# First pair's q and k in 1536-byte rows, turned by products with the identity, its clusters in two halves

## Chip, cores and metric

The kernel runs on one core of a Trainium2 chip. The metric is the device time of one execution in microseconds (us), the median of several runs; "profiled execution" means one further run that the hardware profiler recorded. The engines are TensorE (PE; its weight loads are listed apart as PEld), VectorE (DVE), ScalarE (ACT), GpSimd (POOL) and SyncE (SP), which issues most DMAs.

## What is computed

Attention in which a query sees only the keys of its own cluster, followed by a mixture of experts in which each token goes to one expert. Shapes: 4 batches, 8 heads, 768 tokens, head width 64, 16 centroids per head; the attention's output, as 3072 rows of 512, goes to 8 experts (512 to 1024 to 512).

```python
q_assign = argmax(einsum('bhsd,hcd->bhsc', q_n, c_n)); k_assign likewise   # unit vectors
mask   = q_assign[:, :, :, None] == k_assign[:, :, None, :]
scores = where(mask, q @ k.T / sqrt(64), -1e9)
attn   = softmax(scores) @ v                       # reshaped to x: (3072, 512)
logits = x @ w_gate; e = argmax(logits); gate = softmax(logits)[e]
out    = gate * (relu(x @ w1[e]) @ w2[e])
```

## The kernel before

**Attention.** The 32 (batch, head) pairs are done two heads at a time: 16 "pairs", numbered n. Each has 768 tokens, worked on as two halves of 384 query columns (h = 0, 1) and six blocks of 128 keys (j = 0 to 5). For a pair:

- `load(n)` fetches q and k, `load_v(n)` fetches v. For n > 0 the rows come as quarters of 32 that `turn` (L277, DVE, 32 x 32 block transposes) turns into qT and kT, head width along the partitions, tokens along the columns. For n = 0 the tokens come in another layout, with DMAs on SP and ACT (L183), and PE turns them by 12 transposes (L267); `first_turn` copies the result out of PSUM (L282), half by DVE and half by ACT.
- `similar` (L312, PE): products with the normalised centroids cT (made at L248 to L257 from `cin`, turned by PE at L270, copied at L291).
- `assign0` to `assign2` (L325 to L348, DVE, seven instructions): the largest similarity of each token, ties to the first, as a one-hot row `ohT`.
- `place(n, 1)` (L361, DVE, four instructions) writes the keys' one-hot rows, scaled by a huge number and shifted, into `mk`; `place(n, 0)` (L359, ACT, for n = 0 also POOL) copies the queries' into `mq`. A product of mk and mq adds 0 where the clusters agree and a huge negative number elsewhere.
- `score(n, h, j)`: `score_half` twice on PE (L379), first kT with qT in fp32, then mk with mq in bf16 into the same PSUM tile `sps` (three such tiles); then ACT's exp into A (L392). Before the first score of all, three fp32 halves are issued ahead.
- `add_up` (L398, DVE) sums A over j, `attend` (L404, PE) multiplies by v, `sum_up` (L427, PE) makes the row sums and the gate's logits from `wgt`, `rows` and `store` write x out.

**Order.** Within the attention part each engine runs its instructions in the order in which the program writes them. The main loop, for each n, issues the loads of n + 2, then the twelve scores; after score u (u = h * 6 + j) it calls what a table, filled by `at_pair(n, u, ...)`, holds for that place: the preparation of pair n + 1 in five steps (1 similar, 2 assign0 and assign1, 3 assign2, 4 place keys, 5 place queries), and the work left from pair n - 1. Then come the products with v, in whose middle DVE turns q and k of pair n + 2. Pair 0's five steps run ahead of the loop, one after the other. `routing_constants` (POOL memsets, and SP's DMAs that fill `tokens_of` from `none`, L141) comes after them.

**SP's queue before**: q, k of pair 0 (half of each; ACT issues the other halves, and `cin` and `wgt`); the store of the centroids `c_normed` (waits for cT); v of pair 0; q, k, v of pair 1; eight `tokens_of`; loads of pair 2.

**Experts.** The second part gathers rows by expert and multiplies them in fp32 (L916, L1017, L1036). The change doesn't touch it.

Of the kernel before, what the change touches and what calls it, by code (L numbers as in the profile page):

```python
# [8 lines left out]
F32 = mybir.dt.float32  # L9
BF16 = mybir.dt.bfloat16  # L10
# [3 lines left out]
ALU = mybir.AluOpType  # L14
# [19 lines left out]
def kernel(  # L34
# [45 lines left out]
    cn_d = nc.dram_tensor("c_normed", (H, D, C), F32, kind="Internal").ap()  # L80
# [82 lines left out]
    with tc.manual_schedule(), ExitStack() as actx:  # L163
# [96 lines left out]
        first = []  # L260
        cps = ps_m.tile([P, 512], F32, name="mps")
        for d in (QIN, KIN):
            ps = ps_s.tile([P, 2, 512], F32, name="sps")
            t = d.pop(0)
            for j in range(NQ):
                c0 = P * (j % 3)
                nc.tensor.transpose(ps[:, j // 3, c0 : c0 + P], t[:, j].rearrange("p a d -> p (a d)"), ident)  # L267
            first.append(ps)
            if d is QIN:
                nc.tensor.transpose(cps[:, 0:P], cn.rearrange("p a d -> p (a d)"), ident)  # L270

        QT, KT, SIM, OH = {}, {}, {}, {}

# [2 lines left out]
            dst[n] = qkt.tile([P, S], F32, name=name)  # L276
            nc.vector.transpose(dst[n], src.pop(n).rearrange("p i d -> p (i d)"))  # L277

        def first_turn(w):
            t = (QT, KT)[w][0] = qkt.tile([P, S], F32, name=("qT", "kT")[w])  # L280
            for ins in (
                nc.vector.tensor_copy(t[:, 0:HS], first[w][:, 0, 0:HS]), nc.scalar.copy(t[:, HS:S], first[w][:, 1, 0:HS])  # L282
            ):
                ins = getattr(ins, "ins", ins)
                tc.declare_no_dep(ins, group=f"first_turn{w}", reason="disjoint columns")
                tc.add_to_no_dep_group(f"first_turn{w}", ins)

        first_turn(0)
        cv = cps[:, 0:P].rearrange("p (h a c) -> p h a c", a=2, c=C)
        for a in range(2):  # L290
            nc.vector.tensor_copy(cT[D * a : D * (a + 1), :, a, :], cv[D * a : D * (a + 1), :, a, :])  # L291
        for a in range(2):
            nc.sync.dma_start(
                out=cn_d.rearrange("(h a) d c -> a d h c", a=2)[a], in_=cT[D * a : D * (a + 1), :, a, :]
            )

        load_v(0)
        load(1)
        first_turn(1)
        first_cb = consts.tile([P, C], BF16)  # L300
        nc.gpsimd.tensor_copy(first_cb, first_c)
        ksc2 = consts.tile([P, 2], F32)
# [14 lines left out]
                )  # L317
            SIM[n] = ps

        G = 2 * HI  # L320

        def assign0(n):

            sim = asg.tile([P, HI, 2 * C], F32, name="sim")
            nc.vector.transpose(sim.rearrange("p i c -> p (i c)"), SIM.pop(n)[:, 0:HS])  # L325
            SIM[n] = sim.rearrange("p i (a c) -> p (i a) c", c=C)

        def assign1(n):
            sim = SIM[n]
            mx = asg.tile([P, G], F32, name="mx")  # L330
            nc.vector.tensor_reduce(mx, sim, axis=AX, op=ALU.max)
            ge = asg.tile([P, G, C], BF16, name="ge")
# [3 lines left out]
        def assign2(n):  # L336
            ge = SIM.pop(n)
            rank = asg.tile([P, G, C], BF16, name="rank")
            nc.vector.tensor_tensor(rank, ge, first_cb[:, None, :].to_broadcast([P, G, C]), op=ALU.mult)
            top = asg.tile([P, G], BF16, name="top")  # L340
            nc.vector.tensor_reduce(top, rank, axis=AX, op=ALU.max)
            oh = asg.tile([P, HI, 2 * C], BF16, name="oh")
# [4 lines left out]
            OH[n] = asg.tile([P, HS], BF16, name="ohT")  # L347
            nc.vector.transpose(OH[n], oh.rearrange("p i c -> p (i c)"))  # L348

        def place(n, w):  # L350
            t, m = OH[n], (MQ, MK)[w][n % 2]
            for h in range(2):
                for a in range(2):
                    g = 2 * w + h
                    dst = m[D * a : D * a + Q4, HS * h : HS * (h + 1)]
                    src = t[Q4 * g : Q4 * (g + 1), :]
                    if w == 0:

                        (nc.gpsimd.tensor_copy if n == 0 and h else nc.scalar.copy)(dst, src)  # L359
                    else:  # L360
                        nc.vector.tensor_scalar(  # L361
                            dst, src, scalar1=ksc2[Q4 * g : Q4 * (g + 1), a : a + 1],
                            scalar2=kscn2[Q4 * g : Q4 * (g + 1), a : a + 1], op0=ALU.mult, op1=ALU.add,
                        )
            if w == 0:
                OH.pop(n)


        A, ACC, O, OT, SL = {}, {}, {}, {}, {}
# [3 lines left out]
        def score_half(n, h, j, first):  # L373
            if first:
                SP[n, h, j] = ps_s.tile([P, 2, 512], F32, name="sps")
            kt, qt = (KT[n], QT[n]) if first else (MK[n % 2], MQ[n % 2])
            for a in range(2):
                rows = slice(D * a, D * (a + 1))
                nc.tensor.matmul(  # L379
                    SP[n, h, j][:, a, 0:HS], lhsT=kt[rows, j * P : (j + 1) * P], rhs=qt[rows, h * HS : (h + 1) * HS],  # L380
                    start=first, stop=not first,
                )

        def score(n, h, j):

            ahead = range(3) if n + h + j == 0 else (j,) if n + h or j > 2 else ()
            for i in ahead:
                score_half(n, h, i, True)
# [3 lines left out]
            nc.scalar.activation(A[n, h, j], ps[:, :, 0:HS], AF.Exp, scale=D**-0.5)  # L392
# [1067 lines left out]
```

## Time and profile before

| what | us |
|---|---|
| three timed runs | 671.42, 668.75, 671.11 (median 671.11) |
| the profiled execution's own time | 672.25 |
| its span, from first to last instruction | 670.7 |
| PE busy / DVE busy / ACT busy / POOL busy | 649.9 / 512.3 / 300.0 / 127.3 |
| mean granted TensorE clock | 0.992 |
| one pair in the steady state (first product with v to the next pair's) | 19.74 |

The profile's page gives each engine's busy time, the chain of work that ended last, and the costliest groups of instructions. Lines of the order of time read: start, length, engine, source line, operation, tile written <- tiles read, shape, count, and in brackets the idle time of the engine before it and what ended it. Matmuls are pipelined: a group's length includes the last one's way through the array, and a fp32 product is listed as two records. The groups that the change is about lie in the first 40 us.

| group, pair 0 unless said | first start | us | instructions |
|---|---|---|---|
| PE L267 transposes of q / of k | 5.24 / 6.94 | 1.52 / 1.52 | 6 / 6 |
| DVE L282 copies of qT / kT halves | 6.80 / 8.49 | 0.56 / 0.56 | 1 / 1 |
| DVE L325 to L348 clusters | 10.67 | 4.03 to the end of ohT | 7 |
| DVE L361 mk | 14.81 | 2.03 | 4 |
| ACT L392 first exp | 16.35 | 0.81 each | 12 |
| PE L404 products with v | 27.32 | 7.89 | 48 records |

### The profile page before, as it was taken

The page shows a single profiled execution, that of the slowest core. Times are in us where ns is not written, and L with a number is a line of the kernel's source. Part 1 is how long each engine was busy: PE and PEld are TensorE (multiplying, and loading weights), DVE is VectorE, ACT ScalarE, POOL GpSimd, SP SyncE. Part 2 cuts the span into 40 slices and gives each one's busy share as a digit, 9 for nine tenths or more (in the row PEclk, how much of TensorE's full clock was granted, in tenths as well). Part 3 has the DMA queues.
Part 4 walks back from the last instruction along what each step waited for, and adds up shares of the span by engine and source line. Part 5 has one row for each costly group of instructions (what it writes and reads, how often), then busy time and mean ns, then how long its engine had stood idle before and what let it go on. Part 6 is the DMA issues. An engine that isn't in the chain of part 4 may idle for free.

```text
span 670.7 us, 11366 instructions
## 1 busy us (share of the span) xinstructions
PE 649.9 (97%) x4210; PEld 425.7 (63%) x4210; DVE 512.3 (76%) x901; ACT 300.0 (45%) x522; POOL 127.3 (19%) x156
## 2 busy tenths in 40 slices
PE   5999999999999999999999999999999999999995
PEld 2444444454444455444575879989798887969773
DVE  5889999999999999999886868878778366572300
ACT  3666556657556565556622333243332331423210
POOL 4100000012000300033104704225240422130010
PEclk9899999999999999999999989999999999999998
DMA  6843455433455443347475586685675844625010
GB/s 118 191 86 72 82 95 95 66 73 72 77 95 95 65 81 73 70 115 239 115 266 142 189 297 217 253 321 156 275 239 229 261 160 138 221 93 182 8 48 18
DMA packets 191806, 95.36 MB, mean 142 GB/s; under 512 B 155967, under 2 KB 173887, under 8 KB 190464
## 3 DMA queue, kind: packets, MB, share of 16 engines
q1 hardware_dynamic: 184560, 81.15, 44.0%
q0 software_dynamic: 4928, 12.97, 5.8%
q8 instruction: 35, 0.57, 0.4%
q10 hardware_dynamic: 2256, 0.44, 0.4%
q14 instruction: 27, 0.22, 0.1%
HBM read 74.10 MB, written 20.70 MB: 141 GB/s over the span
## 4 chain that ended last, share of the span: by engine, by line
PE 77%; issue 9%; DVE 7%; POOL 2%; DMA 2%; ACT 1%; POOLq 0%; SPq 0%; DVEq 0%; ACTq 0%
PE sps L379 20%; PE mps L404 15%; PE bank L916 9%; PE sbank L916 7%; PE bank L1017 7%; PE bank L1036 7%; PE sbank L1017 5%; PE mps L427 2%; PE mps L312 2%; DMA xg<-x_rows,gi 1%; PE bank L885 1%; DVE acc L398 1%; DVE v L736 1%; DVE xT L727 1%; POOL tokens_of L554 1%
## 5 line engine op out<-in xcount | busy, mean ns | idle before, releaser
L392 ACT ACTIVATE A<-sps 128x768 f32<-128x768 f32 x192 | 153.5, 811 | 44.9 <-PE sps L379 44.1
L379 PE MATMUL sps<-qT,kT 64*128 64x384 f32 x768 | 159.3, 494 | 0.6 <-ACT A L392 0.6
L398 DVE TENSOR_TENSOR acc<-acc,A 128x768 f32<-128x768 f32 x128 | 121.4, 948 | 10.1 <-ACT A L392 2.8
L404 PE MATMUL mps<-A,v_in 128*64 128x384 f32 x768 | 127.4, 488 | 0.0
L379 PEld LDWEIGHTS sps<-qT,kT 64*128 64x128 f32 x768 | 67.1, 188 | 55.0 <-issue 51.4
L404 PEld LDWEIGHTS mps<-A,v_in 128*64 128x64 f32 x768 | 53.8, 137 | 70.5 <-issue 61.7
L991 POOL DMA_INDIRECT out_dram<-z,si x30 | 47.6, 1587 | 198.4 <-DVE z L874 169.3
L554 POOL DMA_INDIRECT tokens_of<-tg,pos_i x24 | 26.7, 1111 | 281.9 <-DVE pos_i L552 148.2
L379 PE MATMUL sps<-mq,mk 64*128 64x384 bf16 x384 | 63.5, 325 | 2.6 <-DVE mk L361 2.6
L1036 PE MATMUL bank<-w,h 128*128 128x512 f32 (+2 forms) x224 | 64.4, 596 | 0.0
L685 POOL DMA_INDIRECT xg<-x_rows,gi x30 | 42.7, 1423 | 48.2 <-DVE si L676 18.1
L359 ACT COPY mq<-ohT 32x384 bf16<-32x384 bf16 x62 | 31.6, 510 | 42.7 <-DVE ohT L348 41.8
L916 PE MATMUL sbank<-xc,a 128*128 128x144 f32 (+4 forms) x288 | 48.0, 310 | 0.2
L916 PE MATMUL bank<-xT,w 128*128 128x144 f32 (+4 forms) x288 | 47.8, 309 | 0.0
L874 DVE TENSOR_TENSOR h<-sbank,p 128x288 f32<-128x288 f32 (+4 forms) x18 | 9.2, 512 | 48.3 <-PE sbank L916 48.3
L916 PEld LDWEIGHTS bank<-xT,w 128*128 128x128 f32 x288 | 43.8, 191 | 2.6 <-issue 2.2
L1036 PEld LDWEIGHTS bank<-w,h 128*128 128x128 f32 (+2 forms) x224 | 24.7, 152 | 32.5 <-issue 32.3
L916 PEld LDWEIGHTS sbank<-xc,a 128*128 128x128 f32 x288 | 43.3, 191 | 0.9 <-ACT sbank L940 0.6
L379 PEld LDWEIGHTS <-mk 64*128 64x128 bf16 x384 | 19.5, 95 | 28.0 <-DVE mk L361 3.4
L934 ACT ACTIVATE h<-h 128x288 f32<-128x288 f32 (+4 forms) x36 | 17.6, 488 | 42.7 <-DVE h L874 42.5
L702 DVE TENSOR_TENSOR xw<-xg,sf 128x256 f32<-128x256 f32 (+2 forms) x60 | 32.8, 606 | 1.8 <-DMA xg<-x_rows,gi 1.6
L398 DVE TENSOR_TENSOR acc<-A 128x768 f32<-128x768 f32 x32 | 30.2, 945 | 3.1 <-ACT A L392 2.9
(208 smaller groups left out, 890.7 us busy)
## 6 DMA issues: line engine op xcount, KB each, us to landing
w<-in_moe_w_dram SPq DMA_DIRECT2D x20, 2048.0 KB, 12.0
v_in<-in_v_dram SPq DMA_DIRECT2D x32, 192.0 KB, 2.8
x_rows<-x SPq DMA_DIRECT2D x64, 96.0 KB, 2.4
turn_rows<-xw SPq DMA_DIRECT2D x23, 256.0 KB, 2.0
q_in<-in_q_dram SPq DMA_DIRECT2D x60, 96.0 KB, 3.2
k_in<-in_k_dram SPq DMA_DIRECT2D x60, 96.0 KB, 3.2
xs<-turn_rows SPq DMA_DIRECT2D x16, 144.0 KB, 2.8
xs<-turn_rows SPq DMA_DIRECT2D x8, 208.0 KB, 4.2
```

The lines of the kernel that those rows point to most:

```text
L359: (nc.gpsimd.tensor_copy if n == 0 and h else nc.scalar.copy)(dst, src)
L379: nc.tensor.matmul(SP[n, h, j][:, a, 0:HS], lhsT=kt[rows, j * P : (j + 1) * P], rhs=qt[rows, h * HS : (h + 1) * HS], start=first, stop=not ...
L392: nc.scalar.activation(A[n, h, j], ps[:, :, 0:HS], AF.Exp, scale=D**-0.5)
L398: nc.vector.tensor_tensor(ACC[n, h], first, A[n, h, j], op=ALU.add)
L404: nc.tensor.matmul(O[n, h][D * a : D * (a + 1), 0:HS], lhsT=VIN[n][:, a, j, :], rhs=A[n, h, j][:, a, :], start=(j == 0), stop=(j == NQ - 1),)
L554: ins = nc.gpsimd.indirect_dma_start(out=t_d[:, :], out_offset=bass.IndirectOffsetOnAxis(ap=pos_i[:, i : i + 1], axis=0), in_=tg[:, b, i, ...
L685: nc.gpsimd.indirect_dma_start(out=xg[0:m], out_offset=None, in_=x_d[0:rows_in, :], in_offset=bass.IndirectOffsetOnAxis(ap=g["gi"][0:m, j ...
L702: nc.vector.tensor_tensor(xw[0:m, :, :, d2 * a : d2 * (a + 1)], xg[0:m].rearrange("p (r a d b) -> p a r b d", r=HP, a=2, b=DB)[:, a], g["s ...
L916: nc.tensor.matmul(ps[:, f * T2 : (f + 1) * T2], lhsT=w[:, k, (2 * j + f) * P : (2 * j + f + 1) * P], rhs=x[:, k, :], start=first and f + ...
L991: ins = nc.gpsimd.indirect_dma_start(out=out[:, :], out_offset=bass.IndirectOffsetOnAxis(ap=GR[s]["si"][0:rows, j : j + 1], axis=0), in_=z ...
L1017: nc.tensor.matmul(ps[:, 0:H], lhsT=x[:, k, :], rhs=y[:, k, :], start=first and k == 0, stop=k == 3, skip_group_check=not first,)
L1036: nc.tensor.matmul(ps[i * m : (i + 1) * m, :], lhsT=h[:, f, j * P : j * P + m], rhs=w[:, f, :], start=(k == 0), stop=(k == FB // n - 1),)
```

## The change

Line numbers in the diff are those of the changed kernel's hunks; the main pieces:

- **Loads of pair 0.** One DMA for q and one for k, both on SP, with 1536 contiguous bytes per partition and head (before: 256 bytes per partition, head and token block). `load_v(0)` and `load(1)` are issued directly behind, ahead of the constants; `wgt` goes to SP's queue too, and the store of `c_normed` comes last.
- **Turning.** In place of transposes of 128 x 128 blocks (both heads at once), each head's block of 64 columns is the weight of a product with the identity, whose result lands in that head's half of the partitions: 24 products in four groups (q first half, k first half, q second half, k second half), each copied out by ACT.
- **Clusters in halves.** `similar_half`, the seven DVE instructions and the placing are done for 384 tokens at a time (192 columns), first for tokens 0 to 383, then for the rest. The first half's `mq` is copied by ACT (two) and POOL (two), the second half's by POOL alone (four).
- **Order.** The three fp32 score halves that run ahead are issued between the two halves' work: one before `similar_half(1)`, two after. For n = 0, steps 1 to 4 of pair 1's preparation move from places 4, 5, 7, 8 to 6, 7, 8, 9.
- One DVE instruction fewer in the centroids' norm.

```diff
                 if n == 0:
-                    t = d[n] = t.rearrange("p i d -> p (i d)").rearrange("p (j a d) -> p j a d", a=2, d=D)
-                    for a in range(2):
-                        (nc.sync, nc.scalar)[a].dma_start(out=t[:, :, a, :], in_=src[0, a].rearrange("(p j) d -> p j d", j=NQ))
+                    t = t.rearrange("p i d -> p (i d)").rearrange("p (a e) -> p a e", a=2)
+                    nc.sync.dma_start(out=t, in_=src[0, 0:2].rearrange("a (p j) d -> p a (j d)", j=NQ))
+                    d[n] = t.rearrange("p a (j d) -> p a j d", d=D)
                     continue
...
         load(0)
+        load_v(0)
+        load(1)
...
-            nc.scalar.dma_start(
+            nc.sync.dma_start(
                 out=wgt[D * a : D * (a + 1), :, E * a : E * (a + 1)],
...
-        nc.vector.tensor_tensor(cinv, cinv, cs2, op=ALU.mult)
-        nc.vector.tensor_tensor(cinv, cinv, cnrm, op=ALU.add)
+        nc.vector.tensor_scalar(cinv, cinv, scalar1=cs2[:, 0:1], scalar2=cnrm[:, 0:1], op0=ALU.mult, op1=ALU.add)
...
-        def assign0(n):
+        def assign0(n, part=1):
-            sim = asg.tile([P, HI, 2 * C], F32, name="sim")
-            nc.vector.transpose(sim.rearrange("p i c -> p (i c)"), SIM.pop(n)[:, 0:HS])
+            sim = asg.tile([P, HI, 2 * C], F32, name="sim")[:, 0 : HI // part]
+            nc.vector.transpose(sim.rearrange("p i c -> p (i c)"), SIM.pop(n)[:, 0 : HS // part])
...
+        def start_first():
+            HQ = HS // 2
+            cps = ps_m.tile([P, 512], F32, name="mps")
+            ps = [ps_s.tile([P, 2, 512], F32, name="sps") for _ in range(2)]
...
+            def turned(w, h):
+                for j in range(NQ // 2):
+                    for a in range(2):
+                        nc.tensor.matmul(
+                            ps[w][D * a : D * (a + 1), h, P * j : P * (j + 1)], lhsT=src[w][:, a, NQ // 2 * h + j, :], rhs=ident,
+                            start=True, stop=True,
+                        )
+            def copied(w, h):
+                nc.scalar.copy(dst[w][:, HS * h : HS * (h + 1)], ps[w][:, h, 0:HS])
+            def similar_half(h):
+                sps = SIM[0] = ps_m.tile([P, 512], F32, name="mps")
+                for g in range(4):
+                    c0 = HS * h + HQ * (g % 2)
+                    nc.tensor.matmul(
+                        sps[Q4 * g : Q4 * (g + 1), 0:HQ], lhsT=cT[:, 0].rearrange("p a c -> p (a c)"),
+                        rhs=dst[g // 2][:, c0 : c0 + HQ], start=True, stop=True,
+                    )
+            def place_half(h, w):
...
+                        if w == 0:
+                            (nc.gpsimd.tensor_copy if h or g else nc.scalar.copy)(to, OH[0][rows])
+                        else:
+                            nc.vector.tensor_scalar(
+                                to, OH[0][rows], scalar1=ksc2[rows, a : a + 1], scalar2=kscn2[rows, a : a + 1],
+                                op0=ALU.mult, op1=ALU.add,
+                            )
+            def clusters(h):
+                assign0(0, 2)
+                assign1(0, 2)
+                assign2(0, 2)
+                place_half(h, 1)
+                place_half(h, 0)
+
+            turned(0, 0)
+            copied(0, 0)
+            turned(1, 0)
+            copied(1, 0)
+            nc.tensor.transpose(cps[:, 0:P], cn.rearrange("p a d -> p (a d)"), ident)
...
+            turned(0, 1)
+            copied(0, 1)
+            similar_half(0)
+            turned(1, 1)
+            copied(1, 1)
+            clusters(0)
+            score_half(0, 0, 0, True)
+            similar_half(1)
+            for j in (1, 2):
+                score_half(0, 0, j, True)
+            clusters(1)
...
-            for u, step in ((2 if n else 4, 1), (5, 2), (7, 3), (8, 4), (11, 5)):
+            for u, step in ((2 if n else 6, 1), (5 if n else 7, 2), (7 if n else 8, 3), (8 if n else 9, 4), (11, 5)):
                 at_pair(n, u, prepare, n + 1, step)
...
-        for step in range(1, 6):
-            prepare(0, step)
+        start_first()
         routing_constants()
         prepare(1, 0)
```

More of the change, by code (lines that the diff above doesn't have):

```diff
@@ L258 @@
         )
[L260 to L270, printed above, removed]
         QT, KT, SIM, OH = {}, {}, {}, {}
@@ L277, in turn @@
             nc.vector.transpose(dst[n], src.pop(n).rearrange("p i d -> p (i d)"))
[L279 to L299, printed above, removed]
         first_cb = consts.tile([P, C], BF16)
@@ L318, in similar, with assign1, assign2 @@
             SIM[n] = ps
-        G = 2 * HI
-        def assign0(n):
-            sim = asg.tile([P, HI, 2 * C], F32, name="sim")
-            nc.vector.transpose(sim.rearrange("p i c -> p (i c)"), SIM.pop(n)[:, 0:HS])
+        def assign0(n, part=1):
+            sim = asg.tile([P, HI, 2 * C], F32, name="sim")[:, 0 : HI // part]
+            nc.vector.transpose(sim.rearrange("p i c -> p (i c)"), SIM.pop(n)[:, 0 : HS // part])
             SIM[n] = sim.rearrange("p i (a c) -> p (i a) c", c=C)
-        def assign1(n):
+        def assign1(n, part=1):
+            G = 2 * HI // part
             sim = SIM[n]
-            mx = asg.tile([P, G], F32, name="mx")
+            mx = asg.tile([P, 2 * HI], F32, name="mx")[:, 0:G]
             nc.vector.tensor_reduce(mx, sim, axis=AX, op=ALU.max)
-            ge = asg.tile([P, G, C], BF16, name="ge")
+            ge = asg.tile([P, 2 * HI, C], BF16, name="ge")[:, 0:G]
             nc.vector.tensor_tensor(ge, sim, mx.unsqueeze(2).to_broadcast([P, G, C]), op=ALU.is_ge)
             SIM[n] = ge
-        def assign2(n):
+        def assign2(n, part=1):
+            G = 2 * HI // part
             ge = SIM.pop(n)
-            rank = asg.tile([P, G, C], BF16, name="rank")
+            rank = asg.tile([P, 2 * HI, C], BF16, name="rank")[:, 0:G]
             nc.vector.tensor_tensor(rank, ge, first_cb[:, None, :].to_broadcast([P, G, C]), op=ALU.mult)
-            top = asg.tile([P, G], BF16, name="top")
+            top = asg.tile([P, 2 * HI], BF16, name="top")[:, 0:G]
             nc.vector.tensor_reduce(top, rank, axis=AX, op=ALU.max)
-            oh = asg.tile([P, HI, 2 * C], BF16, name="oh")
+            oh = asg.tile([P, HI, 2 * C], BF16, name="oh")[:, 0 : HI // part]
             nc.vector.tensor_tensor(
@@ L346, in assign2 @@
             )
-            OH[n] = asg.tile([P, HS], BF16, name="ohT")
+            OH[n] = asg.tile([P, HS], BF16, name="ohT")[:, 0 : HS // part]
             nc.vector.transpose(OH[n], oh.rearrange("p i c -> p (i c)"))
@@ L357, in place @@
                     if w == 0:
-                        (nc.gpsimd.tensor_copy if n == 0 and h else nc.scalar.copy)(dst, src)
+                        nc.scalar.copy(dst, src)
                     else:
@@ L366, in place @@
                 OH.pop(n)
+        def start_first():
+            HQ = HS // 2
+            cps = ps_m.tile([P, 512], F32, name="mps")
+            ps = [ps_s.tile([P, 2, 512], F32, name="sps") for _ in range(2)]
+            src = [d.pop(0) for d in (QIN, KIN)]
+            dst = [qkt.tile([P, S], F32, name=name) for name in ("qT", "kT")]
+            QT[0], KT[0] = dst
+            def turned(w, h):
[16 more added lines that the diff above has]
+            def place_half(h, w):
+                for g in (2 * w, 2 * w + 1):
+                    for a in range(2):
+                        c0 = HS * h + HQ * (g % 2)
+                        to = (MQ, MK)[w][0][D * a : D * a + Q4, c0 : c0 + HQ]
+                        rows = slice(Q4 * g, Q4 * (g + 1))
+                        if w == 0:
[16 more added lines that the diff above has]
+            nc.tensor.transpose(cps[:, 0:P], cn.rearrange("p a d -> p (a d)"), ident)
+            cv = cps[:, 0:P].rearrange("p (h a c) -> p h a c", a=2, c=C)
+            for a in range(2):
+                nc.vector.tensor_copy(cT[D * a : D * (a + 1), :, a, :], cv[D * a : D * (a + 1), :, a, :])
+            turned(0, 1)
[9 more added lines that the diff above has]
+            clusters(1)
+            OH.pop(0)
+            for a in range(2):
+                nc.sync.dma_start(
+                    out=cn_d.rearrange("(h a) d c -> a d h c", a=2)[a], in_=cT[D * a : D * (a + 1), :, a, :]
+                )
@@ L384, in score @@
         def score(n, h, j):
-            ahead = range(3) if n + h + j == 0 else (j,) if n + h or j > 2 else ()
-            for i in ahead:
-                score_half(n, h, i, True)
+            if n + h or j > 2:
+                score_half(n, h, j, True)
             score_half(n, h, j, False)
```

## The prediction

> **What bounds the kernel now.** I read the page's first part, then the chain that ended last between 10 and 60 us, then the engines' order of time there, then busy time by stretch. The page first:
>
> ```profile
> span 670.7 us, 11366 instructions
> PE 649.9 (97%) x4210; PEld 425.7 (63%) x4210; DVE 512.3 (76%) x901; ACT 300.0 (45%) x522; POOL 127.3 (19%) x156
> PE 77%; issue 9%; DVE 7%; POOL 2%; DMA 2%; ACT 1%; POOLq 0%; SPq 0%; DVEq 0%; ACTq 0%
> ```
>
> TensorE (PE) is full nearly everywhere, so a change to the start is worth what it brings forward the moment from which PE never waits again. The chain shows that moment (start, length, what):
>
> ```profile
> 10.67 0.59 DVE sim L325
> ...
> 14.12 0.59 DVE ohT L348
> ...
> 15.40 0.53 DVE mk L361
> ...
> 16.35 0.82 ACT A L392
> ...
> 17.21 2.80 PE sps L379 x12
> 20.01 1.44 PE mps L312 x8
> 21.45 5.87 PE sps L379 x42
> 27.32 7.89 PE mps L404 x48
> 35.21 2.62 PE sps L379 x18
> ```
>
> Up to 16.35 the start hangs on VectorE (DVE): it makes the first pair's clusters, and the first exp A waits for the masks. From 17.21 all is PE. PE begins pair 0's products with v at 27.32, and its next pairs follow every 19.74 us. So I work out when 27.32 comes in the changed kernel, and whether the gain lasts.
>
> Two more readings. In order of time:
>
> ```profile
> 5.24 1.52 PE L267 MATMUL sps<-ident,q_in 128*128 128x128 f32 x6 [5.24 <-POOL first_cb L301]
> 8.38 1.50 PE L312 MATMUL mps<-qT,cT 128*32 128x384 f32 x4
> 18.45 0.98 DVE L277 STREAM_TRANSPOSE kT<-k_in 128x768 f32<-128x768 f32 x1 [0.60 <-DMA k_in<-in_k_dram]
> 35.99 0.94 DVE L277 STREAM_TRANSPOSE kT<-k_in 128x768 f32<-128x768 f32 x1
> 38.77 0.49 PE L312 MATMUL mps<-qT,cT 128*32 128x384 f32 x2
> ```
>
> The last two are one hand-over: DVE has pair 2's kT at 36.92 and PE wants it at 38.77, 1.85 us of slack, for DVE is nearly as full as PE. And by stretch (PE, weight loads, DVE, ACT, POOL busy, PEclk, DMA share, GB/s):
>
> ```profile
> 14.63:18.04 3.41, 1.82 (x12) 0.78 (x14) 2.98 (x6) 2.71 (x5) 2.97 (x11) 1.00 0.95 172
> 18.04:21.45 3.41, 3.41 (x20) 0.94 (x16) 2.79 (x4) 2.04 (x3) 2.17 (x29) 0.50 1.00 345
> ```
>
> After PE's pause it was granted half its clock for 3.41 us. Full clock would have done that work in half the time, so the stretch cost up to 1.7 us; of it some 1.55 lay on the chain (scores L379 and similar L312; the rest fell in waits for ACT).
>
> **The change, part by part.**
>
> *Loads.* Each of q and k came in two DMAs of 192 KB in rows of 256 B, half from SP, half from ACT. q's ACT half was issued at 1.24 and took 3.9 us, landing at 5.14; PE started at 5.24. The releaser named, first_cb, is a guess of the profile's, since ident was made by 2.26. Now one DMA of 384 KB from SP in rows of 1536 B. The nearest rows are v's two DMAs (192 KB, 1536 B rows): the second, issued 0.65 after the first, landed 2.6 later, so 384 KB in 3.25. Issued at 0.81, q lands between 3.4 (one such DMA) and 4.1; I take 3.7 and PE at 3.8, 1.4 earlier. k, issued at 1.45, lands by 4.7, ahead of its turn. v, pair 1's q and k, wgt and the store of c_normed now follow on SP's queue without waiting for cT; pair 1's loads start some 7 us earlier, which removes the 0.60 that DVE waited for k_in. wgt, needed near 34, loses nothing. ACT, free of four issues, loads its first table earlier, but cnrm still waits for cs2 at 3.11; that and one DVE instruction fewer (0.16 plus a gap) move cn from 5.57 to about 5.4, and PE wants it at 6.4: nothing.
>
> *Turning.* Six transposes took 1.52, 0.22 apart. They become four groups of six products, 64 weight columns by 128, two records each. Nearest row: L404, the same form 384 wide, both halves of the partitions in turn: 7.89 / 24 products = 0.33 each, which is two at a time (L312's records lie 0.32 apart at full clock). A third as wide: 0.22 a pair, 0.66 a group; twice that at half clock. Which clock? L312 at 8.38 took 1.50 for what comes in 0.32 + 0.49 at 38.77, so the start ran at half, though PEclk says 1.00 there. I take half: 1.3 a group; bounds 0.66 and, if pairs do not overlap, 2.6. q's first half 3.8 to 5.1, k's to 6.4, cn to 6.6, q's second half to 7.9, then similar_half: four products 192 wide side by side, 0.64 at half clock, and the 0.28 that lay between L312 and DVE before: sim at 8.8 instead of 10.67. At full clock 8.0; with no overlap 12.7.
>
> *Clusters in halves.* Nothing shows a half instruction, but the L277 row, 0.98 for 768 columns, against sim's 0.58 for 384 gives 0.40 per 384 and 0.18 fixed. The seven instructions halve to 0.38, 0.35, 0.36, 0.26, 0.35, 0.36, 0.38 = 2.44, with gaps 2.8 (whole: 4.1). Four mk instructions took 2.03; halved I take 1.3 with gaps (bounds: 1.0 exact halves, 2.0 no saving). So the first masks of keys stand at about 12.2, and the first exp starts at about 12.6 instead of 16.35. But DVE now does 2 x (2.8 + 1.3) = 8.2 instead of 6.2, and all masks stand at 8.8 + 8.2 = 17.0: before, 16.84. **DVE's front does not move; only its order does.**
>
> [...]
>
> *Scores.* ACT runs exps 0 to 2 from 12.6 to 15.0 while DVE makes the second half. Score 3 needs the second half's first two mk, 16.3; its exp starts at 16.7 instead of 18.45. PE then has eight scores at 0.81 (their spacing at full clock) and similar of pair 1, moved behind score 6, 0.65: 16.5 + 6.5 + 0.65 = 23.6 against 27.32. **3.7 us, if PE keeps its clock.** It pauses again, from about 14.0 to 16.3; the pause that cost half a clock before was 12.9 to 15.4. I take the same window again, 1.3 of cost (bounds 0 and 1.7): 24.9, gain 2.4.
>
> [...]
>
> *DVE behind it.* From mk on, DVE works without a pause of note to kT of pair 2. It gains only the DMA wait and loses the 0.2: kT of pair 1 ends at 17.0 + 1.8 = 18.8 instead of 19.43, kT of pair 2 at 36.3 instead of 36.92. PE, 3.7 earlier, would want it at 35.1 and stand until 36.35. **So the gain is cut to 38.77 - 36.35 = 2.4 on this side also.** The move of similar (pair 1) and of its assign steps by two places changes DVE's order, not its sum. From pair 2 on DVE needs 18.2 of 19.74, so it keeps up and the gain is carried.
>
> *POOL and SP.* POOL makes six half copies instead of two whole (0.49 each; 0.33 by the same slope): the four of the second half run 15.7 to 17.1, needed by PE at 18.1. Its memset none, and behind it SP's eight tokens_of and pair 2's loads, come about 1.2 later (17.1 for 15.87). k of pair 2 was issued until 27.94 and needs some 3.2: 32.4, against DVE's 34.4. Cost nothing; with that cover gone the excess would be DVE's.
>
> **Sum.** Span 670.7 - 2.4 = 668.3; the profiled run was 672.25, so 669.9 of its kind, but the three timed runs stand at 671.11, 1.1 below it. Against their median: **668.7 us**, 0.36% less. What a measurement of this kernel can tell from no change is about 0.5%, 3.4 us, for its own runs lie 2.7 apart.
>
> **The rivals.**
> 1. *The whole 3.7 and more comes.* For it: the clock might hold (a window that falls otherwise), the turning might run at full clock (sim 0.8 earlier, and so DVE's front), mk might halve exactly (0.6 earlier): gain 2.4 + 0.8 + 0.6 = 3.8, 667.3. Against: 1.85 us of slack is read plainly, and all must come together.
> 2. *The start is not earlier*: PE waits for first_cb as the profile names it, and begins at 5.24. Everything is 1.4 later: gain 1.0, 670.1. Against: q's landing at 5.14 explains it as well, and ident is long done.
> 3. *DVE becomes the bound and the kernel slower.* Place: from the second half's mk to similar of pair 2. If products do not overlap, sim comes at 12.7, 3.9 later than I take; all masks stand at 20.9, kT of pair 2 at 40.2, past PE's 38.77: 1.5 slower, 672.6. It decides once sim is later than 8.8 + 2.4 = 11.2. A second half-clock window or DVE's pairs with extra work (20.81 instead of 19.74 at attention's pairs 5 and 9) could add 1 to 2. Against: L404 overlaps the same form.
>
> **How the numbers follow.** Forecast 0.48, its own range 667.2 to 669.9 (clock cost 0 to 1.7, turning clock), a sixth of it past 0.5%; rival 1 0.30; rival 2 0.12; rival 3 0.10. Faster by over 0.5% (under 667.75): 0.30 + 0.08 = 0.38. Slower by over 0.5%: most of rival 3 with its additions, 0.09. The rest, 0.53, lies within. The range runs from rival 1 with the bounds of q's landing, 666.2, to rival 3's near end, 672.0.
>
> **What would show it.** Right: PE's first product at 3.8, first exp at 12.6, a gap between exps 2 and 3 until 16.7, products with v from 24 to 25, the slack before similar of pair 2 near zero, pairs still 19.74 apart. Wrong: products of one group 0.4 apart instead of pairs; a first product at 5.2; DVE's mk done by 16 (rival 1) or after 19 (rival 3); a gain at 40 us that is gone at 280.

## The result and the profile after

The changed kernel took **671.45 us** (median of 14 runs, 669.07 to 674.47), the kernel before on the same chip 671.85 us (14 runs, 668.75 to 674.75). The ratio is **0.9995, 95% interval 0.9975 to 1.0014**: no difference that can be told. The forecast was 668.7 us, a gain of 2.4 us.

The page of the changed kernel's profiled execution (672.44 us):

```profile
span 670.6 us, 11470 instructions
PE 651.2 (97%) x4254; PEld 426.6 (64%) x4254; DVE 512.2 (76%) x909; ACT 299.9 (45%) x524; POOL 133.1 (20%) x160
PE 74%; DVE 16%; DMA 4%; issue 3%; SPq 2%; ACT 0%; DVEq 0%; POOL 0%; POOLq 0%; ACTq 0%
```

Span and busy times are close to those of before (670.7; PE 649.9, DVE 512.3). The change is in the first 40 us, so I look there. The chain of waits (start, length, what):

```profile
0.81 3.54 DMA q_in<-in_q_dram
...
9.25 0.40 DVE sim L292
...
13.22 0.33 DVE mk L374
...
13.58 0.39 DVE sim L292
...
16.82 0.36 DVE mk L374
...
17.22 4.25 PE sps L422 x19
21.47 0.92 PE mps L281 x8
22.39 4.24 PE sps L422 x30
26.63 7.89 PE mps L446 x48
```

The start now hangs on the load of q, then on DVE through *both* halves of the clusters. The first masks come 3 us sooner than before. Yet PE starts its last unbroken stretch at 17.22, now behind DVE, where before it started at 17.21, behind ACT's first exp. From there PE needs 9.4 us to the first product with v, and needed 10.1 before. In order of time on PE and ACT:

```profile
4.48 1.55 PE L348 MATMUL sps<-ident,q_in 128*64 128x128 f32 x12 [4.48 <-DMA q_in<-in_q_dram]
5.78 1.53 PE L348 MATMUL sps<-ident,k_in 128*64 128x128 f32 x12
...
14.12 0.92 PE L422 MATMUL sps<-qT,kT 64*128 64x384 f32 x4
16.84 0.71 PE L422 MATMUL sps<-mq,mk 64*128 64x384 bf16 x2 [1.80 <-DVE mk L374]
...
26.56 7.96 PE L446 MATMUL mps<-A,v_in 128*64 128x384 f32 x48
```

```profile
13.26 2.23 ACT L434 ACTIVATE A<-sps 128x768 f32<-128x768 f32 x3 [0.53 <-PE sps L422]
17.59 1.62 ACT L434 ACTIVATE A<-sps 128x768 f32<-128x768 f32 x2 [2.10 <-PE sps L422]
```

Three exps run early, then ACT idles 2.10 us and PE 1.80 us until the second half's masks. What that pause does is seen in busy time by stretch (PE, weight loads, DVE, ACT, POOL, each with its count; then PEclk, DMA share, GB/s), first the changed kernel, then a second profiled execution of the same kernel:

```profile
14.91:18.32 3.41, 1.56 (x12) 0.89 (x12) 3.04 (x9) 1.31 (x2) 1.68 (x6) 1.00 0.02 5
18.32:21.74 3.42, 3.42 (x17) 1.65 (x17) 3.28 (x4) 1.93 (x4) 3.16 (x10) 0.50 0.50 176
21.74:25.15 3.41, 3.41 (x28) 1.67 (x22) 3.14 (x4) 2.29 (x4) 3.25 (x6) 1.00 0.68 197
```

```profile
13.98:17.39 3.41, 2.14 (x12) 0.59 (x9) 3.00 (x10) 2.23 (x3) 0.00 (x0) 1.00 0.08 11
17.39:20.80 3.41, 2.80 (x11) 1.82 (x13) 3.25 (x7) 1.10 (x2) 2.86 (x12) 0.50 0.03 11
20.80:24.22 3.42, 3.42 (x16) 1.53 (x16) 3.11 (x5) 1.84 (x3) 3.21 (x6) 0.50 0.77 271
```

In both executions the grant of the clock changes here only at the ends of such stretches of 3.41 us (at 18.32 and 21.74 in the first, at 17.39 and 24.22 in the second); below they are called windows, and their ends edges. In the first execution, PE ran the window that follows the pause at half its clock. In the second it ran *two* windows at half, and its first product with v came at 28.90, 1.6 later than before the change. The gain at the start is thus 0.7 us in one execution and a loss in another.

### The profile page after: what moved, and what is told of

It is laid out like the page before. It is cut to its first block, busy times and chain, and to the rows that moved or that the text cites. A ratio compares the mean times of both kernels' runs of the same rounds, so it can differ in the third digit from the quotient of the medians.

```text
span 670.6 us, 11470 instructions
## 1 busy us (share of the span) xinstructions
PE 651.2 (97%) x4254; PEld 426.6 (64%) x4254; DVE 512.2 (76%) x909; ACT 299.9 (45%) x524; POOL 133.1 (20%) x160
## 4 chain that ended last, share of the span: by engine, by line
PE 74%; DVE 16%; DMA 4%; issue 3%; SPq 2%; ACT 0%; DVEq 0%; POOL 0%; POOLq 0%; ACTq 0%
PE sps L422 17%; PE mps L446 13%; PE bank L957 10%; PE sbank L957 8%; PE bank L1058 8%; PE bank L1077 7%; PE sbank L1058 6%; DVE acc L440 5%; PE mps L469 2%; PE mps L281 1%; DVE a L778 1%; DMA xg<-x_rows,gi 1%; PE bank L926 1%; DMA sf<-tokens_of 1%; DVE xT L769 1%
```

## The experiments

"Mark" below is the start of the first product with v (27.25 before, by its first record; the chain puts it at 27.32). Single times are of single executions; ratios rest on 12 runs of the kernel against 17 or 23 of the one before on the same chip. The chips differ between rounds, so ratios and not medians are compared.

### Both kernels again, unchanged

> The kernel before, unchanged, profiled once more. It tells how far the marks of the start repeat: pair 0's first product with v at 27.25 us, similar of pair 2 at 38.77, the half-clock window from 18.04 to 21.46. If the clock's window falls at random, the window moves by up to 3.4 us and the first mark by up to 1.6; if it falls at a fixed place, all three return within 0.4.

> The changed kernel, unchanged, profiled once more: first product with v at 26.56, similar of pair 2 at 38.08, half clock from 18.33 to 21.74. Theory A (the start gained 0.7 us in truth): the first mark is 0.4 to 1.0 below that of the kernel before. Rival (0.7 is where the clock's window happened to fall): it lies anywhere from 2.4 below to 0.5 above.

> The changed kernel unchanged, once more. Theory: first product 4.5 to 4.9, first sim 9.2 to 10.4 by when full clock comes, a pause of PE of 1.8 us between the first and the second half's masks, then none, one or two windows of 3.41 us at half clock by how the pause lies to the windows' edges, so the first product with v at 25.1 to 26.0, 26.5 to 27.5, or 28.4 to 29.2. The pause of some 2.4 us between 380 and 390 us is followed by half clock if it lies whole in one window and not if an edge cuts it in two parts that are both over half a us. Rival (the two runs seen differ for another cause): windows and edges don't go together.

| us | forecast | after | after_third | after_again | before | before_again |
|---|---|---|---|---|---|---|
| first turning product or transpose | 3.8 | 4.48 | 4.72 | 4.82 | 5.24 | 5.34 |
| first sim on DVE | 8.8 | 9.25 | 9.21 | 10.40 | 10.67 | 10.71 |
| first exp | 12.6 | 13.26 | 13.22 | 14.41 | 16.35 | 16.38 |
| all masks of keys | 17.0 | 17.93 | 17.89 | 19.09 | 16.84 | 16.87 |
| exp of score 3 | 16.7 | 17.59 | 17.55 | 18.91 | 18.45 | 18.63 |
| half clock before 30 us | one window | 18.32 to 21.74 | 17.91 to 21.33 | 17.39 to 24.22 | 18.04 to 21.46 | 17.91 to 21.32 |
| mark | 24.9 | 26.56 | 26.58 | 28.90 | 27.25 | 27.33 |
| time | | 672.44 | 671.23 | 671.61 | 672.25 | 672.05 |

The kernel before repeats itself to 0.2 us; the changed one has two courses. In the worse one full clock first came at 10.56 instead of 8.09 and 7.67, so the turning ran at half clock but for its last group (1.55, 1.52, 1.55 and 1.00 us), everything stood 1.2 us later, and the pause of 1.8 us was followed by two windows at half. The mean of the three marks, 27.35, is that of before, in line with the 14 timed runs. Three executions are few, and the two of the kernel before are more alike than they need be: an edge lies at 11.22 in one and at 11.08 in the other. They don't show what that kernel does when the edges fall elsewhere.

### PE kept busy in the pause

Three products that nobody reads, with the identity as weights, in the pause of each kernel:

```diff
+            if (n, h, j) == (0, 0, 3):      # kernel before: n + h + j == 0
+                busy = ps_m.tile([P, 512], F32, name="mps")
+                for _ in range(3):
+                    nc.tensor.matmul(busy[:, 0:HS], lhsT=ident, rhs=QT[0][:, 0:HS], start=True, stop=True)
                 score_half(n, h, j, False)
```

> The changed kernel with three products of 0.64 us more, whose result nothing reads, between score 3's two halves, where TensorE waits from 14.8 to 16.8 us for the masks. Theory C (the half clock after this pause takes most of what the change should have given): no half-clock window near 18, first product with v at 24.9 to 25.2, so 1.4 to 1.7 earlier, and the whole 1.0 to 1.7 us shorter. Rival D (VectorE's later front sets the pace, whatever the clock): the first product comes earlier, but similar of pair 2 still waits for kT at 36.7 and the gain there is 1.4 at most. Rival N (the clock doesn't depend on this pause): window and marks as before.

> The kernel before with the same three products in its pause, 12.9 to 15.4 us, ahead of the first mask product. Theory C: no half-clock window near 18, first product with v at 25.6 to 25.9 instead of 27.25; VectorE, whose work is unchanged, has pair 2's kT at 36.9 and stops similar of pair 2 there, so 1.6 to 1.8 earlier than 38.77. Rival N: as before, 27.2 or later by what the three products push back.

The changed kernel with them: **0.997 (0.9955 to 0.9985)**, no half-clock window before 30 us, mark 25.95. This in an execution whose start was as late as that of after_again (full clock at 10.49, first sim 10.27, score 3's exp 18.61 against 18.91). Score 3's exp to mark took 7.34; it took 9.99 in after_again and 8.97 in the first profile. So one window cost 1.63 us and two cost 2.65. Busy time of that execution by stretch:

```profile
13.90:17.32 3.42, 3.35 (x16) 1.46 (x14) 3.05 (x9) 2.24 (x3) 0.00 (x0) 1.00 0.07 10
17.32:20.73 3.41, 3.41 (x23) 1.89 (x21) 3.25 (x7) 2.12 (x3) 2.93 (x12) 1.00 0.05 18
```

PE is full through the pause, and the window after it has its whole clock. Unread work on the busiest engine left the kernel faster than the one before, and in the trace the clock is the difference that it made. Against the changed kernel without them (0.9975 to 1.0014) the intervals overlap, so that step by itself is at the edge of the noise. Without a halved window, score 3's exp to mark takes 7.33 to 7.35 in three more profiles below, and 7.62 in after_lateload, whose kT came late.

The kernel before with them: mark 26.04, no window either, yet a ratio of 1.0013 (0.9998 to 1.0029). That profile's mark is 1.2 earlier and its own execution took 671.14, 1.1 less than the first of the kernel before; the median of the 12 runs shows no such gain. Why stays open.

### The parts of the change alone

after_lateload moves v's and pair 1's loads back behind the centroids; halves_alone keeps only the clusters in halves, with the loads and transposes of before; after_whole keeps loads and products, with whole clusters and pair 1's preparation at its old places.

```diff
 # after_lateload, and so in halves_alone
         load(0)
-        load_v(0)
-        load(1)
...
                 nc.vector.tensor_copy(cT[D * a : D * (a + 1), :, a, :], cv[D * a : D * (a + 1), :, a, :])
+            for a in range(2):
+                nc.sync.dma_start(
+                    out=cn_d.rearrange("(h a) d c -> a d h c", a=2)[a], in_=cT[D * a : D * (a + 1), :, a, :]
+                )
+            load_v(0)
+            load(1)
...
 # halves_alone, in turned(w, h); its loads of q, k and wgt are those of the kernel before
-                    for a in range(2):
-                        nc.tensor.matmul(
...
+                    nc.tensor.transpose(
+                        ps[w][:, h, P * j : P * (j + 1)], src[w][:, NQ // 2 * h + j].rearrange("p a d -> p (a d)"), ident
+                    )
...
 # after_whole, in start_first
-            similar_half(0)
             turned(1, 1)
             copied(1, 1)
-            clusters(0)
-            score_half(0, 0, 0, True)
-            similar_half(1)
-            for j in (1, 2):
+            for step in range(1, 4):
+                prepare(0, step)
+            for j in range(3):
                 score_half(0, 0, j, True)
-            clusters(1)
-            OH.pop(0)
+            place(0, 1)
+            place(0, 0)
```

> The changed kernel with v of pair 0 and all of pair 1's loads back behind the store of c_normed, so that nothing but cin, q and k is in flight at the start. Theory Q (a load of 384 KB at the start takes 3.7 to 4.0 us to land by itself): TensorE's first product stays at 4.5 to 4.8 us. Rival (the loads issued behind it slow it): first product at 3.7 to 4.0, and cin's first use by VectorE back from 3.3 to 2.7.

> Clusters in halves and the new order, but the loads in 256 B rows from two queues and their queue order as before, and the turning by transposes, three a group. Theory P (products at half clock give back what the earlier load brings): first TensorE instruction at 5.3, a group of three in 0.7 us, VectorE's first sim at 9.0 to 9.5, as early as in the changed kernel or earlier, masks of all tokens at 17.3 to 17.9, first product with v at 26 to 27 with a half-clock window. Rival (loads and products together are worth what I took, 1.4 minus 0.4 us): sim at 10.2 or later.

> Loads and products as in the changed kernel, but the clusters whole, placed as before, and pair 1's preparation at its old places. If halving is the part that pays: sim at 11.0 (clock up early) to 12.2 (late), all masks 6.2 later at 17.2 to 18.4, first exp at 16.7 to 17.9, first product with v at 27.5 to 29, later than the 27.25 and 27.33 of the kernel before. If halving is a loss as VectorE's 2 us more work suggests: first product with v before 26.5.

| us | after_lateload | halves_alone | after_whole |
|---|---|---|---|
| first product or transpose | 4.61 | 5.17 | 4.90 |
| first sim | 10.02 | 9.52 | 11.66 |
| all masks of keys | 18.71 | 18.20 | 17.83 |
| pauses of PE over 0.5 us from 12 to 20 us | 1.81 | 0.60 and 1.04 | 2.65 |
| half clock before 30 us | none | none | 16.19 to 23.02 |
| mark | 25.99 | 25.21 | 29.04 |
| time of the one run | 672.32 | 671.18 | 674.53 |

Three readings. First, **q's landing is the load's own**: with the other loads away PE still began at 4.61. The view of DMA traffic, 40 slices of the first 10 us, shows part of the reason (changed kernel, then after_lateload):

```profile
GB/s 0 0 0 0 0 0 0 84 69 55 148 365 393 393 399 393 399 356 356 356 369 387 311 221 223 206 183 149 104 125 139 160 115 131 130 161 140 137 139 130
```

```profile
GB/s 0 0 0 0 0 0 0 69 56 74 144 318 398 399 393 399 412 328 230 107 16 0 0 0 0 0 0 0 0 0 0 0 0 0 0 0 0 14 52 0
```

From 1.75 to 2.75 us 55 to 148 GB/s are moved, and only then close to 400. The forecast took its 3.25 us for 384 KB from v's loads at 9 us. By the chain it took 3.54, from the issue at 0.81 to 4.35, past the later of my bounds for q's landing (3.4 and 4.1). Part of that stays open: by the slices 384 KB had been moved by some 3.5 us, PE began at 4.48, and k's load follows q's at once in both runs, so whether k holds q back isn't tested.

Second, **the loads and products alone are a loss, by the marks**: with whole clusters the first sim comes at 11.66, 1.0 later than before, though PE started 0.4 sooner. Four groups, all but the last at half clock (1.55, 1.52, 1.49 and 0.82 us), 1.3 us and more apart, stand where two of 1.5 us stood, and a whole sim needs all of q and k. Its pause of 2.65 us was followed by two windows at half clock, and the mark is the latest of all; how much of that is the fall of the windows, one execution can't tell.

Third, halves_alone reached a mark of 25.21 with no new load and no products, where 26 to 27 with a halved window was expected. Its PE, at half clock until 12.35 (four score records in 1.65 us at 10.21, eight in 1.56 at 12.50), was late with the three fp32 halves, so that its pause fell into two short ones and no window was halved. How often that happens, one execution doesn't show. Without added products this version was not timed further, so that the halves alone do better than the whole change isn't ruled out.

### Full clock early as well

Five products of the identity with itself ahead of the turning, with the three in the pause: in the changed kernel, in the kernel before, and in halves_alone.

```diff
+            early = ps_m.tile([P, 512], F32, name="mps")
+            for _ in range(5):
+                nc.tensor.matmul(early[:, 0:P], lhsT=ident, rhs=ident, start=True, stop=True)
             turned(0, 0)
```

> The kernel after_keep with five products of the identity with itself ahead of the first product, from 2.3 us on, while q is on its way; their result is read by nothing. Theory: TensorE counts as busy from 2.3, its full clock comes by 9 at the latest (it came between 8.1 and 10.6), sim at 8.9 to 9.3 instead of 9.3 to 10.4, first product with v at 24.6 to 25.2 against 25.95 in after_keep, and the whole 0.5 to 1.2 us below after_keep's ratio of 0.997. Rival (VectorE's front at pair 2 takes it): similar of pair 2 follows kT at once and the total equals after_keep's within 0.3.

> The kernel before with five early products and the three in its pause. Theory (halves and clock each hold a part): full clock earlier, first sim near 9.5 instead of 10.07 to 10.7, all masks near 15.7, no window at half clock before 30 us, first product with v at 25.3 to 25.7, ratio 0.998 to 1.001. Rival (the clock is all, the halves are nothing): ratio 0.997 or less, as the changed kernel with the same products.

> The clusters in halves with the loads and transposes of before, and with five early products and the three in the pause, so that the clock is out of the comparison. Theory (the 1536 B rows and the products bring nothing of themselves): first transpose of q near 5.2 as before, first sim 8.8 to 9.4, all masks of keys by 17.8, no window at half clock after the pause, first product with v at 24.4 to 25.2, ratio to before 0.995 to 0.998, like the changed kernel with the same products (0.9962). Rival (the earlier load is what the change lives on): first sim after 9.8, first product with v after 25.5, ratio 0.999 or more.

| | changed | before | halves_alone |
|---|---|---|---|
| full clock from | 6.04 | 8.51 | 11.58 |
| first sim | 8.48 | 10.07 | 9.62 |
| mark | 24.17 | 26.32 | 25.58 |
| median of 12 runs | 669.33 | 671.13 | 671.45 |
| ratio to before | **0.9962** | 0.9988 | 0.9991 |
| 95% | 0.9947 to 0.9978 | 0.9974 to 1.0002 | 0.9977 to 1.0005 |

PE of the changed kernel so fed, in order of time:

```profile
2.31 2.50 PE L388 MATMUL mps<-ident 128*128 128x128 f32 x10 [2.31 <-POOL ident masks.py:199]
4.75 1.49 PE L348 MATMUL sps<-ident,q_in 128*64 128x128 f32 x12
6.06 0.82 PE L348 MATMUL sps<-ident,k_in 128*64 128x128 f32 x12
...
14.20 2.20 PE L437 MATMUL mps<-qT,ident 128*128 128x384 f32 x6
16.34 0.46 PE L425 MATMUL sps<-mq,mk 64*128 64x384 bf16 x2
...
24.17 7.96 PE L453 MATMUL mps<-A,v_in 128*64 128x384 f32 x48
```

It runs from 2.31 to the mark with hardly a gap, k's group already at full clock (0.82 for 1.53). It has the lowest ratio of all versions timed, though its interval overlaps that of after_keep; against the changed kernel itself (0.9995) the difference of 0.0033 is larger than the two half intervals combined as independent (0.0025). The same in halves_alone:

```profile
2.31 2.50 PE L383 MATMUL mps<-ident 128*128 128x128 f32 x10 [2.31 <-POOL ident masks.py:199]
5.29 0.87 PE L344 MATMUL sps<-ident,q_in 128*128 128x128 f32 x3 [0.48 <-DMA q_in<-in_q_dram]
6.95 0.88 PE L344 MATMUL sps<-ident,k_in 128*128 128x128 f32 x3 [0.79 <-DMA k_in<-in_k_dram]
```

With loads shared out over two queues in 256 B rows PE begins on q at 5.29 and on k at 6.95, after waits of 0.48 and 0.79, for 4.75 and 6.06 without such waits in the changed kernel, and full clock comes at 11.58 for 6.04. My theory here, that the new rows and products bring nothing of themselves, gave 0.995 to 0.998; the rival's 0.999 or more came true, with its mark over 25.5, and the sim at 9.62 between the two; the interval just reaches the theory's 0.998. By these traces rows and products together bring a first stage of PE without holes. The kernel before with the same products has full clock at 8.51, its sim at 10.07 where I expected 9.5, its mark at 26.32 where I expected 25.3 to 25.7, and its ratio as expected; the interval leaves out the rival's 0.997, by which the clock would have been all.

Between the changed kernel and the one before, both so fed, the mark differs by 26.32 - 24.17 = 2.15 us and the ratios by 0.0026, or 1.7 us, with intervals that overlap a little. That is near the forecast's 2.4, but not at the same clock: full clock came at 6.04 in one and at 8.51 in the other. With the pause alone filled it came at 10.49 and 8.56, the other way round, and the marks are 25.95 and 26.04. **An estimate at nearly equal clocks is 1.1 us:** the first profile (full clock from 8.09) with 7.34 behind its exp at 17.59 gives 24.93 without a halved window, against 26.04 for before_keep (from 8.56).

## What the second part adds

A gain at the mark is carried to pair 12: the first profile's is 0.69 at 27 us and 0.63 there (265.72 for 266.35). Behind it, it isn't always. From pair 14's first product with v to pair 15's it is 19.1 us in all four profiles of the kernel before (fed or not) and in four of the nine of the changed kernel and its variants, but 19.55 to 19.86 in the other five. The first profile lost its gain there; after_third kept it (335.80 for 336.49 at the first PE product behind attention). after_warm_keep, too, took 19.81: of its 2.15 against before_warm_keep 1.83 is left at pair 1, and 0.67 at pair 15 (326.99 for 327.66). The largest single piece in the first profile is an exp that began late, for which PE stood 0.43; what held ACT isn't shown.

Then comes a part that the change doesn't touch, and there the executions part by more than the gain. PE waits there once for some 2.5 us on VectorE, which makes an input of the experts' products (h). In the kernel before and in after_again, busy time by stretch:

```profile
383.27:386.68 3.41, 0.99 (x9) 0.78 (x7) 3.19 (x4) 0.08 (x1) 2.04 (x2) 1.00 0.69 235
386.68:390.10 3.42, 3.42 (x12) 3.15 (x13) 1.20 (x3) 1.50 (x4) 0.00 (x0) 0.50 0.78 206
```

```profile
382.61:386.03 3.42, 2.84 (x24) 2.62 (x22) 3.28 (x4) 0.79 (x2) 2.81 (x3) 1.00 0.85 285
386.03:389.44 3.41, 1.52 (x11) 1.47 (x11) 2.19 (x4) 1.01 (x3) 0.90 (x1) 1.00 0.32 102
```

The pause is alike, 2.42 us from 384.20 and 2.47 us from 385.45. In the first it lies whole between two edges of the clock's windows, and the next window runs at half. In the second an edge at 386.03 cuts it into 0.58 and 1.90, and no window is halved. So it was in all 13 profiled executions:

| the largest piece of the pause in one window | executions | next window at half clock | experts, first to last product, less PE's own waits |
|---|---|---|---|
| 2.20 to 2.58 us | 7 | 7 | 321.97 to 322.60 us, mean 322.34 |
| 1.38 to 1.90 us | 6 | 0 | 319.8 to 321.1 us, mean 320.56 |

By these means a window at half cost 1.8 us there, and which of the 13 got it went by where an edge fell, not by the kernel. The timed runs agree with this: of the kernel before's 63 in the rounds of the experiments, the 20 with a mean granted clock of 0.993 or less have a median of 672.85, the 43 others 671.01; where in an execution the clock was lower, the mean doesn't tell. PE's waits in that part (4.7 to 7.1 us in the same 13) spread by another 2.4 us. Both are large beside the gain, and 14 runs can't tell one below some 0.2%. The profile of before_keep, whose mark gained 1.2, had 6.64 us of such waits, that of before 4.87.

## Why the prediction was wrong

**Right.** The turning products overlap in pairs (groups 1.30 apart at half clock, as taken; rival 3's doubled price is out). The seven halved DVE instructions take 2.44 us, each as worked out. The first exp is three us sooner, exps 2 and 3 have the gap, PE's pause lies near where it was put (15.04 to 16.84). Pairs follow every 19.74 us. VectorE's front does not move forward. Rival 2 (a start at 5.24) fell: PE began at 4.48 to 4.82. VectorE's cap on the gain is real: in after_warm_keep PE wants pair 2's kT at 35.68 and has it at 35.94, and the next pair follows 20.06 us behind the first instead of 19.74.

**The step that failed: the sum for the first product with v, 24.9.** Each of the three terms that I can tell apart was too small. By how much:

| us more than forecast | after | after_third | after_again |
|---|---|---|---|
| exp of score 3, "its exp starts at 16.7" | 0.89 | 0.85 | 2.21 |
| from there to the mark without a halved window, 23.6 - 16.7 = 6.9 | 0.44 | 0.44 | 0.44 |
| "the same window again, 1.3 of cost (bounds 0 and 1.7)" | 0.33 | 0.39 | 1.35 |
| the mark, 24.9 | 1.66 | 1.68 | 4.00 |

The columns add up by construction, since the windows' cost is what the stretch from exp to mark took (8.97, 9.03, 9.99) over the 7.34 of after_keep.

*Score 3's exp.* This is the largest term. Of the 0.89, 0.45 had come by the first sim (PE's start +0.68, partly won back at full clock); the rest is mostly the halved mk, 1.47 and 1.57 us for 1.3. From first sim to last mask DVE took 8.68 us where I had 8.2, and 6.17 before: so its front did not stay where it was but fell back by 1.1. In after_again PE's start was 1.02 late and the turning ran at half clock up to sim: 1.60 at the first sim.

*To the mark.* In after_keep the 0.44 lies at the places where PE goes from scores to similar, back, and on to the products with v; I had counted the bare spacing.

*The clock.* The windows cost 1.63, 1.69 and 2.65, outside my bounds in the third: two windows had no place in them. I had treated the window as a property of the pause, and had misread its rows. In the kernel before (PE in order of time, then its busy time by stretch):

```profile
15.42 0.33 PE L379 MATMUL sps<-mq,mk 64*128 64x384 bf16 x1 [2.37 <-DVE mk L361]
15.98 0.66 PE L379 MATMUL sps<-mq,mk 64*128 64x384 bf16 x5 [0.22 <-DVE mk L361]
17.21 0.92 PE L379 MATMUL sps<-qT,kT 64*128 64x384 f32 x4 [0.57 <-ACT A L392]
11.22:14.63 3.41, 1.83 (x12) 0.76 (x8) 3.13 (x7) 0.00 (x0) 0.00 (x0) 1.00 0.89 166
```

An edge at 14.63 cut that pause of 2.37 us. The window with its larger piece, 1.58, was followed by full clock; half clock followed the next window, which held the other 0.79 and two short waits. In the three executions of the changed kernel the pause was alike (1.80 to 1.81 us): whole in one window it cost 1.63 and 1.69, cut by the edge at 17.39 into 1.20 and 0.61 it cost 2.65. Full clock first came at an edge too (8.09, 7.67 and 10.56), and the turning's speed, which shifts the start, went by it (0.88 us for a group at full clock, 1.55 at half). The price of this early pause is a spread, not a number. Rival 3 had named a second half-clock window, but only as an addition of its own; it belonged into the forecast's own range.

One sum was wrong without consequence for the forecast: at full clock the prediction's own terms put sim at some 6.6 (3.8 + 3 x 0.66 + 0.2 + 0.32 + 0.28), not at 8.0.

## What to carry to other kernels

Where a trace shows half clock behind a pause, as here (one or two windows, 1.63 to 2.65 us), price the pause as a range over the places where the windows can fall, not as one number; a change that brings work forward but leaves a hole behind it can give much of it back. Here the rearrangement alone (0.9995) and eight unread products alone (0.9988) can't be told from no change; together they gave 0.9962. Before halving a tile on a full engine, add what the second half ends later: here first sim to last mask took 8.68 us for 6.17.

## What the runs showed of the hardware

- PE's clock was granted by windows of 3.413 us on a fixed grid: in the kernel before, the edges at 11.22, 18.04, 21.46, 386.68, 390.10 and 666.58 are whole multiples of it apart (365.22 from 21.46 to 386.68 is 107 windows), and so are 8.09, 18.32, 21.74, 386.96 and 390.38 in the first profile of the changed kernel. The grid's place differed from execution to execution: by the first of these edges, 11.22 and 8.09, it is shifted by 0.28 us.
- From half clock, windows that PE was busy for 3.42 of 3.42 us (7.80 to 11.22, the kernel before), 3.41 of 3.41 (4.68 to 8.09, the changed kernel's first profile) and some 3.2 of 3.41 (5.10 to 8.51, before_warm_keep, busy from 5.30) were followed by full clock. Windows of 2.56 (4.39 to 7.80, the kernel before) and 2.80 (17.39 to 20.80, after_again) were not. From full clock the pause in the experts' part halved the next window at 2.20 us or more in one window (2.20 in halves_warm_keep, 2.42 in the kernel before) and not at 1.90 (after_again). At the start no such line shows: 1.20 us in one window halved the next in after_again, while 1.58 in the kernel before (13.05 to 14.63) did not, and its next window, with 1.58 in three pieces, did. What sets that difference isn't shown.
- Transposes on PE counted as work for the clock: in before_warm_keep the window from 5.10 to 8.51 held almost nothing but transposes, 13 of them from 5.30 on, and the next ran at full clock (the first products of similar took 0.86 us there, and 1.50 in the kernel before, at half clock). In before_keep, without the early products, the like window from 5.15 to 8.56 was 97% busy, and the next ran at full clock too.
- The records of the clock begin with its first rise (8.09 in the changed kernel's first profile, 11.22 in that of before). Ahead of it the 1.00 of the views stands for no record: in the changed kernel the turning groups begun at 4.48 and 5.78 took 1.55 and 1.53 us, the one begun at 9.11 took 0.88.
